# Infini-attention and a spectral filter on one core: other steps for maxima, products, keys and reciprocals, and 14 instead of 15 products in the output projection

## The chip, the cores and the metric

The kernel runs on one core of a Trainium2 chip. A core has several engines that work beside one another, each on its own queue of instructions in program order: TensorE for matrix products (PE in the profile; PEld are its weight loads), VectorE (DVE), ScalarE (ACT), GpSimd (POOL), and SyncE (SP), which here only issues DMA transfers. The engines wait for one another by semaphores. The metric is the device time of a run in microseconds; of several runs the median is given.

## The reference

Two computations share the input size of 2048 x 576 and are written side by side. The first (A) is attention with a compressive memory, with 32 heads of 18 columns and 4 segments of 512 rows:

```python
phi = lambda t: jnp.where(t > 0, t + 1.0, jnp.exp(t))
for s in range(N):                       # 4 segments
    qs, ks, vs = q[:, :, s], k[:, :, s], v[:, :, s]
    logits = jnp.einsum("bhqd,bhkd->bhqk", qs, ks) * scale + mask   # causal
    p = _softmax(logits, axis=-1)
    a_dot = jnp.einsum("bhqk,bhkd->bhqd", p, vs)
    pq = phi(qs)
    num = jnp.einsum("bhld,bhde->bhle", pq, M)
    den = jnp.einsum("bhld,bhd->bhl", pq, z)[..., None] + 1e-6
    o = g * (num / den) + (1.0 - g) * a_dot
    pk = phi(ks)
    M = M + jnp.einsum("bhld,bhle->bhde", pk, vs)
    z = z + jnp.einsum("bhld->bhd", pk)
return o @ wo
```

The second (B) is `irfft2(rfft2(x) * (w_r + 1j*w_i))` over 2048 x 576.

## The kernel before, in words

Up to about 356 us TensorE computes part B as products with Fourier tables, and, between these, the projections of part A to queries, keys and values, which go to DRAM (qkD, vD, pqD). From then on the attention loop runs, `attention`, with t from 0 to 132. A step t handles one head of one segment. k = t // 4 is a quad of four heads, hh = t % 4 the head in it, n = t // 8 a group of eight heads, and g = n // 4 the segment.

Each step interleaves three pieces of work on TensorE. `s1` multiplies queries and keys for a later step (t+10), and VectorE takes the row maxima (L647 a plain reduction over a masked product, L641 a reduction with the mask added in the same instruction, followed by a read of its accumulator). `s2` multiplies again for the step t itself (L682, L686, L687, L691), now with the maximum as two more rows of the query stack, so that ScalarE can take the exponential at once. `pv` multiplies the exponentials by the values, for two steps together (L711).

The maxima go from `s1` to `s2` by `mpath(k)`: VectorE and ScalarE gather them (L659, L660), GpSimd splits them into a high and a low half (mh, L662 and L663), TensorE transposes them (L666), ScalarE copies the result to mts (L669; there is one buffer), and two steps after that a DMA issued by ScalarE puts them into rows 108 and 109 of the query stack (L672, `Qs<-mts`). It is started for the quad k+2 at hh = 1, and its other two pieces are both taken at hh = 3.

Queries and keys of a group of eight heads come as stacks of 108 rows, six loads of 18 rows each (L621, 144 KB). There are three query stacks and four key stacks in turn (the tiles Qs, Ks, and an x that takes over an older buffer). The loads wait in a Python list q, from which two a step are issued on SP, between the smaller transfers: products out (uD, rD; L722, L727), values (L628), pq (L756). The program order of SP is the order of issue. A load of a stack that is to be used again waits until the last product on its old contents.

When a segment g-1 is complete, `recip` (L745, L749) inverts its row sums and sends them through DRAM to a tile rr; `combine` multiplies the products ux, loaded from uD by `ux_load` (L805), by rr (L826, L829, L831), adds the memory's part, and splits the result into a high part oh and a low part ol (L816, L819), in five tiles t = 0 to 4 of 126 rows, the last of 72. `mem1` (L784, L790) computes the memory's part am from pq, `den` (L765) its denominators, and `oproj` (L849) the output projection: for each of 8 units of 128 rows by 288 columns, 15 products, namely oh with the high part of wo, oh with its low part, ol with its high part, for five tiles each. `mixed` runs `combine` and `mem1` in turn. These are generators in a list bg, of which one piece a step (now and then two) is run; `den`, the parts of `recip` and the issue of loads sit in a second list, lane. For segment 3, `last_tile` and `last_proj` do the same at the end.

`late_setup` loads wo in five parts at the start of the loop (L604 on SP, L608, L609), and each wait for a free buffer holds up what SP issues next. Before the loop, `prologue` runs the first ten steps of `s1` between the products of the inverse FFT, and issues the stacks of groups 1 and 2 and the keys of group 3.

Of the kernel before, what the change touches and what calls it, by code (L numbers as in the profile page):

```python
# [102 lines left out]
class FFT:  # L103
# [178 lines left out]
    def inverse(s,yl,pp):  # L282
# [101 lines left out]
class ATT:  # L384
# [210 lines left out]
    def late_setup(s,cp):  # L595

        nc,io=s.nc,s.io; q=[]
        s.sel=cp.tile([96,5,126],BF,name="sel",bufs=1); nc.gpsimd.dma_start(s.sel,io["sel"].rearrange("p (t m) -> p t m",t=5))
        s.woh=cp.tile([126,5,576],F32R,name="woh",bufs=1); s.wol=cp.tile([126,5,576],F32R,name="wol",bufs=1)
        for t in range(6):  # L600
            if t>1: yield
            if t<5:
                x=cp.tile([128,576],F32,name="ob")[:126]; q.append(x)
                nc.sync.dma_start(x,io["wo"][:,576*t:576*t+576])  # L604
            for _ in range(2): yield
            if t>0:
                x=q.pop(0)
                nc.scalar.copy(s.woh[:,t-1],x)  # L608
                nc.gpsimd.tensor_tensor(s.wol[:,t-1],x,s.woh[:,t-1].bitcast(F32),op=OP.subtract)  # L609
        yield  # L610
        yield from s.gates()
    def stack_dmas(s,n,qk):
# [17 lines left out]
    def s1(s,t):  # L630

        nc=s.nc; k,hh=divmod(t,4); n,qd=divmod(k,2); h=4*qd+hh
        Q,K=s.Qs[n%3],s.Ks[n%4]; tp=s.sm
        assert (n,0) in s.loaded and (n,1) in s.loaded,(t,n)
        if hh==0: s.mg[k]=tp.tile([128,4,4],F32,name="mg"); s.mx[k]=tp.tile([128,4,4],F32,name="mx")
        def mm(out,i):
            nc.tensor.matmul(out,Q[:108,h,128*i:128*i+128],K[:108,h,:128*(i+1)],start=True,stop=True)  # L637
        def red(src,i):
            w=128*(i+1)
            junk=tp.tile([128,512],BF,name="junk",bufs=1)  # L640
            nc.vector.tensor_tensor_reduce(out=junk[:,:w],in0=src,in1=s.mask[:,512-w:],scale=1.0,scalar=-3.0e38,  # L641
                op0=OP.add,op1=OP.max,accum_out=s.mg[k][:,hh,i:i+1])
# [4 lines left out]
        nc.vector.tensor_reduce(out=s.mx[k][:,hh],in_=pa.rearrange("p (b c) -> p b c",c=128),axis=mybir.AxisListType.X,op=OP.max)  # L647
# [158 lines left out]
    def combine(s,g):  # L806

        nc=s.nc; tp=s.tp; xs=s.ux
        s.oh=[None]*5; s.ol=[None]*5
        eng=lambda: nc.vector if s.now>=117 else nc.gpsimd  # L810
        yield
        yield
        def high(u):
            r=126 if u<4 else 72
            s.oh[u]=tp.tile([126,512],F32R,name="oh",bufs=5); s.ol[u]=tp.tile([126,512],F32R,name="ol",bufs=5)
            (nc.vector.tensor_copy if s.now>=119 else nc.scalar.copy)(s.oh[u][:r],s.am[u][:r])  # L816
        def low(u):
            r=126 if u<4 else 72
            eng().tensor_tensor(s.ol[u][:r],s.am[u][:r],s.oh[u][:r].bitcast(F32),op=OP.subtract)  # L819
        late=g==2  # L820
        for t in range(7+late):
            if t>1 and not late: high(t-2); low(t-2)
            if t<5:
                r=126 if t<4 else 72; x=xs[t]
                pb=s.post("pb")
                nc.tensor.matmul(pb[:r],s.sel[:,t,:r],s.rc["rr"],start=True,stop=True)  # L826
# [7 lines left out]
            if late and 1<t<7: high(t-2)  # L834
            if late and t>2: low(t-3)
            yield
    def oproj(s,g):
        nc=s.nc
        oh,ol=s.oh,s.ol
        for tb in range(4):  # L840
            ob=s.tp.tile([128,576],F32,name="ob")
            c=slice(128*tb,128*tb+128)
            for hf in range(2):
                ps=(s.ps.tile([128,512],F32,name="po",tag=s.potag) if s.potag else s.post("po"))[:,:288]
                w=slice(288*hf,288*hf+288)
                L=[(a,b,t) for a,b in ((oh,s.woh),(oh,s.wol),(ol,s.woh)) for t in range(5)]
                for i,(a,b,t) in enumerate(L):
                    r=126 if t<4 else 72
                    nc.tensor.matmul(ps,a[t][:r,c],b[:r,t,w],start=i==0,stop=i==14)  # L849
# [42 lines left out]
    def prologue(s):  # L892

        nc,io=s.nc,s.io
        yield
        s.load_v(0)
        q=s.stack_dmas(1,0)+s.stack_dmas(1,1)+s.stack_dmas(2,0)+s.stack_dmas(2,1)+[lambda: s.load_v(1)]+s.stack_dmas(3,1)
        for i in range(2): yield
        i=0
        for t in range(10):  # L900
            for _ in s.s1(t):
                for _ in range(1+(i%24==0)):
                    if q: q.pop(0)()
                i+=1
                yield
            if 2<=t<6: nc.gpsimd.dma_start(s.Ks[t-2][108:110].rearrange("p h c -> p (h c)"),io["neg1"])
            if t in (3,7): m=s.mpath(t//4); next(m)
            if t in (4,8): next(m); next(m,None)
        assert not q
    def homes(s):  # L910

        for n,t,b in (("oh",F32R,5),("ol",F32R,5),("am",F32,5),("pq",F32,5),("ux",F32,3)): s.tp.tile([128 if b==3 else 126,512],t,name=n,bufs=b)
    def attention(s,tp,ps):
        nc=s.nc; s.tp,s.ps,s.psm,s.mtag=tp,ps,s.ps1,"s1"
        s.homes()
# [4 lines left out]
        m=None  # L920
# [12 lines left out]
        for t in range(133):  # L933
            k,hh=divmod(t,4); n,qd=divmod(k,2); g=k//8
            if hh==0 and qd==0:
                if 0<n<14: q+=s.stack_dmas(n+2,0)
                if 0<n<13: q+=s.stack_dmas(n+3,1)
                if n+2<16: q.append(lambda n=n: s.load_v(n+2))
            st=t%32
            if 16<=t<21: s.pq_load(1,t-16)  # L940
            if t==34: bg.append(s.den(1,lane))
            if st==8 and g>0:
                def ln(g=g):
                    r=s.recip(s.rD[g-1],s.rrD[g-1],s.g1,False,"rr",2)
# [12 lines left out]
            if qu: qu.pop(0)()  # L957
# [88 lines left out]
def arrays(x,wq,wk,wv,wo,beta):  # L1046
    f=lambda a: np.asarray(a,np.float32)
    return dict(xa=host_xa(f(x)),wqk=host_wt(np.concatenate([f(wq),f(wk)],1)).reshape(128,-1),wv=host_wt(f(wv)).reshape(128,-1),
        wo=host_wo(f(wo)).reshape(126,-1),beta=np.repeat(f(beta),4).reshape(128,1),**atables())
# [74 lines left out]
```

## Time and profile before

| | us |
|---|---|
| median of 3 runs | 722.68 |
| lowest, highest run | 722.34, 756.58 |
| the profiled execution | 718.92 |
| its span, from the first to the last instruction | 717.2 |
| TensorE busy in that span | 684.1 |
| granted TensorE clock, mean | 0.997 |

The page and the answers of the trace come from the one profiled execution, so that sums are made against its 718.92 us. In its rows L12 is line 12 of the kernel. A row of the timeline gives the start, the duration, the engine, the line, the operation and its tiles (out<-in), and in brackets the idle time ahead of it with what ended it. A row of the groups of waits says which instruction of which line waited for which, with the sum, how often, and the longest. A row of the chain gives the start, the length and the work that was waited for. The table of stretches gives busy times between two points of time.

### The profile page before, as it was taken

The numbers are of one execution on the slowest core, as the hardware profiler recorded it, in microseconds if no ns is written. First come the engines' busy times: TensorE is split into PE (matmuls) and PEld (weight loads), VectorE is DVE, ScalarE is ACT, GpSimd is POOL, SyncE is SP. The second block draws the span as 40 slices with busy tenths as digits, with TensorE's granted clock in tenths as the row PEclk, the third lists the DMA queues.
The fourth block names the chain that finished last, engine by engine and source line by source line (L and its number), as shares of the span: only waits on it lengthen the run. The fifth ranks groups of instructions, "written<-read, shape, count | busy, mean of one in ns | idle before, by whom it ended". The sixth has DMA issues, their size and how long they took to land. (4 is left out here: it accounts for less than half of the span.)

```text
span 717.2 us, 14460 instructions
## 1 busy us (share of the span) xinstructions
PE 684.1 (95%) x5007; PEld 505.7 (71%) x5007; DVE 552.3 (77%) x1270; ACT 450.1 (63%) x985; POOL 211.1 (29%) x403
## 2 busy tenths in 40 slices
PE   4999999999999999999999899899999999999997
PEld 4988869879779879999854444444466445664497
DVE  5999979899699789788588787878466876568633
ACT  3665796585586575444487677767466776567521
POOL 5432000100200111665154333435123662235300
PEclk9999999999999999999999999999999999999999
DMA  8995435645363568899547665776446775441152
GB/s 305 293 280 164 148 118 185 192 169 182 110 220 147 178 198 281 208 231 228 165 111 174 171 172 136 185 173 170 114 126 158 195 169 126 126 137 42 28 153 83
DMA packets 83304, 121.02 MB, mean 169 GB/s; under 512 B 11472, under 2 KB 50750, under 8 KB 83096
## 3 DMA queue, kind: packets, MB, share of 16 engines
q1 hardware_dynamic: 76580, 104.11, 50.3%
q0 software_dynamic: 5632, 15.76, 8.0%
q8 instruction: 39, 0.64, 0.4%
q10 hardware_dynamic: 1020, 0.25, 0.2%
q14 instruction: 33, 0.27, 0.1%
HBM read 81.78 MB, written 38.24 MB: 167 GB/s over the span
## 5 line engine op out<-in xcount | busy, mean ns | idle before, releaser
L641 DVE CUSTOM_DVE_ANT_0 junk<-s,x 128x512 bf16<-128x512 f32 (+1 forms) x256 | 141.4, 552 | 67.2 <-PE s L637 62.0
L696 POOL TENSOR_SCALAR_AFFINE_SELECT P<-P 128x512 f32<-128x512 f32 (+2 forms) x132 | 78.8, 623 | 67.3 <-ACT P L683 51.8
L647 DVE TENSOR_REDUCE mx<-s 128x4 f32<-128x512 f32 x128 | 87.7, 686 | 2.9 <-PE s L646 0.7
L683 ACT ACTIVATE P<-s 128x512 f32<-128x512 f32 x128 | 76.4, 597 | 16.5 <-PE s L682 5.4
L711 PE MATMUL pv<-P,vs 128*32 128x512 f32 (+3 forms) x1024 | 82.8, 441 | 0.0
L692 ACT ACTIVATE P<-s 128x256 f32<-128x256 f32 x128 | 49.4, 386 | 49.7 <-PE s L691 49.6
L688 ACT ACTIVATE P<-s 128x512 f32<-128x512 f32 x128 | 76.1, 594 | 2.0 <-PE s L687 1.8
L637 PE MATMUL s<-Ks,Qs 108*128 108x384 bf16 (+3 forms) x256 | 69.1, 301 | 1.2 <-DVE mx L647 0.9
L711 PEld LDWEIGHTS pv<-P,vs 128*32 128x32 f32 x1024 | 27.2, 109 | 45.3 <-issue 42.5
L459 PE MATMUL pj<-x,wqkh 128*128 128x512 f32 x162 | 56.5, 409 | 0.0
L205 DVE TENSOR_TENSOR Z<-t,t 128x290 f32<-128x290 f32 (+1 forms) x96 | 48.4, 554 | 0.1
L637 PEld LDWEIGHTS <-Qs 108*128 108x128 bf16 x320 | 31.5, 98 | 22.6 <-issue 11.3
L506 POOL MEMSET vt<- 128x32 f32 x16 | 2.4, 166 | 149.1 <-PE pm L516 127.7
L205 DVE TENSOR_TENSOR t<-Z 128x580 f32<-128x580 f32 x64 | 46.0, 755 | 0.0
L142 PE MATMUL f<-ftab,eh 128*128 128x290 f32 (+1 forms) x160 | 32.5, 322 | 12.1 <-DMA ftab<-ftab 9.5
L646 PE MATMUL s<-tri,idb 128*128 128x128 bf16 x256 | 43.2, 220 | 0.0
L295 PE MATMUL i<-civ,Y 128*128 128x256 f32 (+1 forms) x288 | 39.0, 288 | 0.2 <-POOL Y L280 0.2
L295 PEld LDWEIGHTS i<-civ,Y 128*128 128x128 f32 (+1 forms) x288 | 36.4, 181 | 1.0 <-POOL Y L280 0.4
L306 PE MATMUL i<-itab,T 128*128 128x290 f32 (+1 forms) x224 | 36.3, 305 | 0.1
L637 PE MATMUL s<-Ks,x 108*128 108x384 bf16 (+3 forms) x128 | 35.3, 306 | 1.1 <-DVE mx L647 0.6
L142 PEld LDWEIGHTS f<-ftab,eh 128*128 128x128 f32 (+1 forms) x160 | 26.2, 207 | 14.1 <-issue 8.5
L459 PE MATMUL pj<-x,wqkl 128*128 128x512 f32 x90 | 35.5, 395 | 0.0
(203 smaller groups left out, 1820.8 us busy)
## 6 DMA issues: line engine op xcount, KB each, us to landing
qkD<-sp SPq DMA_DIRECT2D x36, 384.0 KB
Ks<-qkD SPq DMA_DIRECT2D x72, 144.0 KB
x<-qkD SPq DMA_DIRECT2D x60, 144.0 KB
Qs<-qkD SPq DMA_DIRECT2D x60, 144.0 KB
xin<-xb SPq DMA_DIRECT2D x16, 384.0 KB
cfw<-cfw POOLq DMA_DIRECT2D x16, 384.0 KB, 4.4
civ<-civ POOLq DMA_DIRECT2D x16, 384.0 KB, 7.6
vs<-vD SPq DMA_DIRECT2D x16, 330.0 KB
```

Source lines behind the costliest of these rows:

```text
L142: nc.tensor.matmul(p[:,r,:FP],x,t,start=n==0,stop=n==6)
L205: v.tensor_tensor(o,a,b,op=op)
L295: nc.tensor.matmul(p[:m,k],Y[i][:,q,c*128:c*128+m],cc[:,hl,o:o+256],start=n==0,stop=n==5)
L459: s.nc.tensor.matmul(out,a,b,start=i==0,stop=i==len(L)-1)
L637: nc.tensor.matmul(out,Q[:108,h,128*i:128*i+128],K[:108,h,:128*(i+1)],start=True,stop=True)
L641: nc.vector.tensor_tensor_reduce(out=junk[:,:w],in0=src,in1=s.mask[:,512-w:],scale=1.0,scalar=-3.0e38, op0=OP.add,op1=OP.max,accum_out=s.m ...
L647: nc.vector.tensor_reduce(out=s.mx[k][:,hh],in_=pa.rearrange("p (b c) -> p b c",c=128),axis=mybir.AxisListType.X,op=OP.max)
L683: nc.scalar.activation(P[0][:,hh],p0,AF.Exp,scale=SC)
L688: nc.scalar.activation(P[1][:,hh],p1,AF.Exp,scale=SC)
L692: nc.scalar.activation(P[2][:,hh],p2,AF.Exp,scale=SC)
L696: nc.gpsimd.affine_select(out=x[:,r],in_=x[:,r],pattern=[[0,r.stop-r.start],[1,128]],compare_op=OP.is_ge,fill=0.0,base=0,channel_multiplie ...
L711: nc.tensor.matmul(s.pvt[32*hh:32*hh+32,128*j:],vt[:,j,19*h:19*h+32],mv[0][:,hh,mv[1]],start=j==0,stop=j>1,skip_group_check=True)
```

## The change

- **Lead.** `s1` runs 11 steps ahead instead of 10, and `prologue` runs 11 steps of it. The keys of group 3 are loaded in the first steps of the loop instead of in `prologue`.
- **Reductions.** In `s1` for t from 11 to 14, the two reductions with the mask inside are plain ones; the mask is added by a product on TensorE.
- **Maxima.** `mpath(k+2)` starts at hh = 0 and its other two pieces are taken at hh = 1, one step later instead of two. The transfer to the query stack is thus issued two steps earlier.
- **Products' loads.** The first three `ux_load` of a segment are issued during three of the steps of `recip` instead of together after them. Tile 4, that of 72 rows, becomes the first in the loads of pq, in `mem1`, in `combine` and in `ux_load`.
- **Denominators.** For segments 2 and 3, `den(g+1)` comes after the first four pieces (two units) of `oproj(g-1)` rather than ahead of it.
- **Projection.** The 72 rows of tile 4 leave 56 free. The tile oh[4] gets 56 rows of the low part below its own, ol[4] becomes oh once more with the remaining 16 rows of the low part below, and the operands of wo are stacked to fit. Tile 4 then takes two products instead of three, and a unit 14 instead of 15. Three transfers within SBUF per segment put the rows in place, one and two steps later. wo is loaded in six parts of 128 rows. Segment 3 keeps its products.

```diff
@@ tables and setup
+ORD=(4,0,1,2,3)
 def host_wo(w):
-    o=np.zeros((126,5,D),np.float32)
-    o[:,:4]=w[:504].reshape(4,126,D).transpose(1,0,2)
-    o[:72,4]=w[504:]
+    o=np.zeros((128,6,D),np.float32)
+    o[:126,:4]=w[:504].reshape(4,126,D).transpose(1,0,2)
+    o[:72,4]=w[504:]; o[72:,4]=w[504:560]; o[72:88,5]=w[560:]
...
-        for t in range(6):
-            if t>1: yield
-            if t<5:
-                x=cp.tile([128,576],F32,name="ob")[:126]; q.append(x)
+        for t in (0,1,2,3,5,4,6):
+            if t: yield
+            if t<6:
+                x=cp.tile([128,576],F32,name="ob"); q.append((t,x))
                 nc.sync.dma_start(x,io["wo"][:,576*t:576*t+576])
...
+                if u==5: nc.scalar.copy(s.wol[64:96,4],x[64:96]); continue
+                r=128 if u<4 else 72
+                nc.scalar.copy(s.woh[:,u],x)
+                nc.gpsimd.tensor_tensor(s.wol[:r,u],x[:r],s.woh[:r,u].bitcast(F32),op=OP.subtract)
@@ s1
         def red(src,i):
             w=128*(i+1)
+            if 11<=t<15:
+                nc.tensor.matmul(src[:,w-128:w],s.idb,s.tri,start=False,stop=True,skip_group_check=True)
+                nc.vector.tensor_reduce(out=s.mg[k][:,hh,i:i+1],in_=src,axis=mybir.AxisListType.X,op=OP.max)
+                return
@@ mixed
-                for _ in s.mem1(g,i-d): yield
+                for _ in s.mem1(g,ORD[i-d]): yield
@@ combine
+            A,B=s.oh[u],s.ol[u]
+            l=B if u<4 else tp.tile([128,512],F32R,name="ol4",bufs=1)
+            eng().tensor_tensor(l[:r],s.am[u][:r],A[:r].bitcast(F32),op=OP.subtract)
+            if u==4:
+                s.later(1,lambda: nc.sync.dma_start(B[:72].bitcast(F32),A[:72].bitcast(F32)))
+                s.later(2,lambda: (nc.sync.dma_start(A[72:128].bitcast(F32),l[:56].bitcast(F32)),nc.sync.dma_start(B[72:88].bitcast(F32),l[56:72].bitcast(F32))))
...
-            if t>1 and not late: high(t-2); low(t-2)
+            if t>1 and not late: high(ORD[t-2]); low(ORD[t-2])
...
-                if t<2: s.later(1,lambda t=t: s.ux_load(g,t+3))
+                if t<2: s.later(1,lambda t=t: s.ux_load(g,ORD[t+3]))
@@ oproj
-                L=[(a,b,t) for a,b in ((oh,s.woh),(oh,s.wol),(ol,s.woh)) for t in range(5)]
+                L=[(a,b,t,126) for a,b in ((oh,s.woh),(oh,s.wol),(ol,s.woh)) for t in range(4)]+[(oh,s.woh,4,128),(ol,s.wol,4,88)]
...
-                    if i==7: yield
+                    if i==6: yield
@@ prologue
-        q=s.stack_dmas(1,0)+s.stack_dmas(1,1)+s.stack_dmas(2,0)+s.stack_dmas(2,1)+[lambda: s.load_v(1)]+s.stack_dmas(3,1)
+        q=s.stack_dmas(1,0)+s.stack_dmas(1,1)+s.stack_dmas(2,0)+s.stack_dmas(2,1)+[lambda: s.load_v(1)]
...
-        for t in range(10):
+        for t in range(11):
@@ attention
-                if 0<n<13: q+=s.stack_dmas(n+3,1)
+                if n<13: q+=s.stack_dmas(n+3,1)
...
-            if 16<=t<21: s.pq_load(1,t-16)
+            if 16<=t<21: s.pq_load(1,ORD[t-16])
...
                     for i in range(8):
+                        if 2<i<6: s.ux_load(g-1,ORD[i-3])
                         next(r); yield
-                    for u in range(3): s.ux_load(g-1,u)
                     yield from r
                     bg.append(s.mixed(g))
-                    if g<3: bg.append(s.den(g+1,lane))
-                    bg.append(s.oproj(g-1))
+                    o=s.oproj(g-1)
+                    if g<3: bg.append(itertools.islice(o,4)); bg.append(s.den(g+1,lane))
+                    bg.append(o)
...
-            a=s.s1(t+10) if t+10<128 else iter(())
+            a=s.s1(t+11) if t+11<128 else iter(())
...
-            if hh==3 and m is not None: steps(m,1)
+            if hh==1 and m is not None: steps(m,1)
             steps(b,1)
-            if hh==3 and m is not None: steps(m,1)
-            if hh==1 and k+2<32: m=s.mpath(k+2); next(m)
+            if hh==1 and m is not None: steps(m,1)
+            if hh==0 and k+2<32: m=s.mpath(k+2); next(m)
```

More of the change, by code (lines that the diff above doesn't have):

```diff
@@ L1 @@
-import math
+import math, itertools
 from contextlib import ExitStack
@@ L598, in late_setup @@
         s.sel=cp.tile([96,5,126],BF,name="sel",bufs=1); nc.gpsimd.dma_start(s.sel,io["sel"].rearrange("p (t m) -> p t m",t=5))
-        s.woh=cp.tile([126,5,576],F32R,name="woh",bufs=1); s.wol=cp.tile([126,5,576],F32R,name="wol",bufs=1)
-        for t in range(6):
-            if t>1: yield
-            if t<5:
-                x=cp.tile([128,576],F32,name="ob")[:126]; q.append(x)
-                nc.sync.dma_start(x,io["wo"][:,576*t:576*t+576])
[L605 to L609, printed above, removed]
+        s.woh=cp.tile([128,5,576],F32R,name="woh",bufs=1); s.wol=cp.tile([128,5,576],F32R,name="wol",bufs=1)
+        for t in (0,1,2,3,5,4,6):
+            if t: yield
+            if t<6:
+                x=cp.tile([128,576],F32,name="ob"); q.append((t,x))
+                nc.sync.dma_start(x,io["wo"][:,576*t:576*t+576])
+            yield
+            if t!=5: yield
+            if len(q)>(t<6):
+                u,x=q.pop(0)
+                if u==5: nc.scalar.copy(s.wol[64:96,4],x[64:96]); continue
+                r=128 if u<4 else 72
+                nc.scalar.copy(s.woh[:,u],x)
+                nc.gpsimd.tensor_tensor(s.wol[:r,u],x[:r],s.woh[:r,u].bitcast(F32),op=OP.subtract)
         yield
@@ L814, in high @@
             r=126 if u<4 else 72
-            s.oh[u]=tp.tile([126,512],F32R,name="oh",bufs=5); s.ol[u]=tp.tile([126,512],F32R,name="ol",bufs=5)
+            s.oh[u]=tp.tile([128,512],F32R,name="oh",bufs=5); s.ol[u]=tp.tile([128,512],F32R,name="ol",bufs=5)
             (nc.vector.tensor_copy if s.now>=119 else nc.scalar.copy)(s.oh[u][:r],s.am[u][:r])
@@ L832, in combine @@
                     eng().tensor_tensor(s.am[t][:r],x[:r],s.am[t][:r],op=OP.add)
-                if t<2: s.later(1,lambda t=t: s.ux_load(g,t+3))
-            if late and 1<t<7: high(t-2)
-            if late and t>2: low(t-3)
+                t=i
+                if t<2: s.later(1,lambda t=t: s.ux_load(g,ORD[t+3]))
+            if late and 1<t<7: high(ORD[t-2])
+            if late and t>2: low(ORD[t-3])
             yield
@@ L845, in oproj @@
                 w=slice(288*hf,288*hf+288)
-                L=[(a,b,t) for a,b in ((oh,s.woh),(oh,s.wol),(ol,s.woh)) for t in range(5)]
-                for i,(a,b,t) in enumerate(L):
-                    r=126 if t<4 else 72
-                    nc.tensor.matmul(ps,a[t][:r,c],b[:r,t,w],start=i==0,stop=i==14)
-                    if i==7: yield
+                L=[(a,b,t,126) for a,b in ((oh,s.woh),(oh,s.wol),(ol,s.woh)) for t in range(4)]+[(oh,s.woh,4,128),(ol,s.wol,4,88)]
+                for i,(a,b,t,r) in enumerate(L):
+                    nc.tensor.matmul(ps,a[t][:r,c],b[:r,t,w],start=i==0,stop=i==13)
+                    if i==6: yield
                 nc.scalar.copy(ob[:,w],ps)
@@ L910, in homes @@
     def homes(s):
-        for n,t,b in (("oh",F32R,5),("ol",F32R,5),("am",F32,5),("pq",F32,5),("ux",F32,3)): s.tp.tile([128 if b==3 else 126,512],t,name=n,bufs=b)
+        for n,t,b in (("oh",F32R,5),("ol",F32R,5),("am",F32,5),("pq",F32,5),("ux",F32,3),("ol4",F32R,1)): s.tp.tile([128 if n in ("oh","ol","ux","ol4") else 126,512],t,name=n,bufs=b)
     def attention(s,tp,ps):
@@ L1048, in arrays @@
     return dict(xa=host_xa(f(x)),wqk=host_wt(np.concatenate([f(wq),f(wk)],1)).reshape(128,-1),wv=host_wt(f(wv)).reshape(128,-1),
[L1049 removed]
+        wo=host_wo(f(wo)).reshape(128,-1),beta=np.repeat(f(beta),4).reshape(128,1),**atables())
 def emit(nc,tc,io):
```

3 lines of the change are left out of this document (1 added, 2 removed).

## The prediction

> **What bounds the kernel now.** I began with the first part of the profile's page (busy time, share of the span and instruction count of each engine), because it says which engine a saving has to reach.
>
> ```profile
> PE 684.1 (95%) x5007; PEld 505.7 (71%) x5007; DVE 552.3 (77%) x1270; ACT 450.1 (63%) x985; POOL 211.1 (29%) x403
> ```
>
> TensorE works for 684.1 us of a span of 717.2, so everything that can be gained by removing waits is 33 us. The next view is the table of stretches: start and end, length, busy time of PE, PEld, DVE, ACT, POOL, granted clock, share of the DMA engines, GB/s.
>
> ```profile
> 250.00:358.00 108.00, 107.37 (x778) 98.26 (x777) 86.61 (x192) 55.24 (x126) 40.15 (x66) 1.00 0.79 221
> 357.00:371.00 14.00, 12.87 (x106) 6.73 (x106) 12.45 (x40) 11.13 (x27) 6.35 (x11) 1.00 0.39 109
> 371.00:402.00 31.00, 28.30 (x259) 14.43 (x258) 24.69 (x79) 22.77 (x56) 14.61 (x25) 1.00 0.71 171
> 434.00:472.00 38.00, 35.22 (x318) 17.61 (x318) 32.32 (x96) 28.05 (x71) 13.97 (x31) 1.00 0.67 162
> 472.00:500.00 28.00, 26.30 (x207) 13.18 (x208) 21.84 (x64) 20.30 (x48) 12.58 (x20) 1.00 0.70 176
> 590.00:650.00 60.00, 59.91 (x515) 38.17 (x508) 38.16 (x112) 38.10 (x92) 19.02 (x40) 1.00 0.46 123
> ```
>
> Before 358 (the FFT) and after 590 TensorE is full: there only less TensorE work is a gain. It idles 1.1 us in 357 to 371, where VectorE is nearly full (12.45 of 14), and 2.7, 2.8 and 1.7 us in the three rows from 371 to 500, where the DMA share is near 0.7. The groups of waits from 358 on say what ended those idle times (microseconds, times, longest).
>
> ```profile
> PEld L682 <- DMA Qs<-mts: 3.7, 3, 1.6
> PE s L682 <- DMA Qs<-mts: 3.2, 3, 1.4
> ACT mts L669 <- DMA Qs<-mts: 2.6, 3, 1.3
> PE pd L765 <- DMA pq<-pqD: 1.4, 1, 1.4
> PE pb L826 <- DMA rr<-rrD: 1.2, 1, 1.2
> PEld L637 <- DMA Qs<-qkD: 1.1, 2, 0.7
> PE s L637 <- DMA Qs<-qkD: 0.4, 1, 0.4
> ```
>
> PEld and PE rows of one line are the same stall twice, so I count PE's 3.2 and a wait of 0.25 us of the same kind at 406.96: about 3.5 us for the maxima. The other two removable waits are 1.4 and 1.2 us. The chain of work that ended last shows the transfers themselves (start, length, what).
>
> ```profile
> 387.69 5.19 DMA pq<-pqD
> 392.89 8.27 DMA Qs<-qkD
> ...
> 460.61 5.79 DMA rr<-rrD
> ...
> 467.94 8.14 DMA Ks<-qkD
> ...
> 481.35 8.42 DMA Qs<-mts
> ...
> 500.58 6.41 DMA pq<-pqD
> ```
>
> A maxima transfer of 8 KB takes 8.42 us, as long as the 144 KB of a query part (8.27). The time is not in the bytes: a transfer stands behind those issued before it. In 371 to 500 the loads are a line in which each new one waits its turn.
>
> **The change part by part.** *Reductions of steps 0 to 3.* They run where VectorE is the limit.
>
> ```profile
> 356.18 0.69 DVE L647 TENSOR_REDUCE mx<-s 128x4 f32<-128x512 f32 x1
> 356.79 0.68 DVE L641 CUSTOM_DVE_ANT_0 junk<-s,x 128x512 bf16<-128x512 f32 x1
> 357.39 0.08 DVE L641 DVE_READ_ACCUMULATOR2_ANT mg<- 128x1 f32 x1
> 357.62 0.42 DVE L641 CUSTOM_DVE_ANT_0 junk<-s,x 128x256 bf16<-128x256 f32 x1
> 357.97 0.69 DVE L647 TENSOR_REDUCE mx<-s 128x4 f32<-128x512 f32 x1
> ```
>
> From start to start, a plain reduction over 512 takes 0.61 us (356.18 to 356.79) and the custom one with its accumulator read 0.83 (to 357.62): 0.22 saved, four times, is 0.9; for the four over 256 (0.35 to the next start) I see nothing to save. Eight mask products are added on TensorE, which idles only 1.1 us there. Range 0 to -0.9; I take **-0.5**.
>
> *Lead 11 instead of 10.* One more step of maxima work goes into the FFT stage and leaves the end of the loop. Both stretches are full on TensorE, so it is the same work at another place: 0. VectorE has room before 358 (86.61 of 108). The six key loads that leave the prologue fall into 357 to 371, where the DMA share is 0.39: 0. But each query stack is now wanted one step sooner, while its loads are put into the queue at the same step as before, since the buffer is free no earlier. Here are the first uses in the program's TensorE order (start, length, operation, idle time before it).
>
> ```profile
> 398.77 0.33 PE L637 MATMUL s<-Ks,x 108*128 108x384 bf16 x1
> 401.64 0.34 PE L637 MATMUL s<-x,Qs 108*128 108x384 bf16 x1
> ...
> 468.58 0.33 PE L637 MATMUL s<-Ks,Qs 108*128 108x384 bf16 x1
> 471.98 0.34 PE L637 MATMUL s<-x,Qs 108*128 108x384 bf16 x1 [0.44 <-DMA Qs<-qkD]
> ```
>
> The first pair is around group 4, the second around group 8. The last query load of group 4 lands at 392.89 + 8.27 = 401.16 in the chain and its stack's first use is at 401.64; at 471.98 the matmul waits for the load itself. There is no spare time at either place. In the changed kernel the step that began at 398.77 wants what lands at 401.2 to 401.6, and the one that began at 468.58 wants what lands near 471.9. If the line of loads moves at its own pace, TensorE is late by 2.4 to 2.9 us at the first and, less the 0.44 already waited and some 0.5 of other work between, by **+2.4** at the second. These are not added: the second is where TensorE stands in relation to the loads, whatever was won earlier. That is the point on which my sum turns: the gains ahead of 472 (0.5 at the start, the maxima at 380, 398 and 407, the 1.2 for rr at 466) are swallowed, because TensorE arrives earlier only to wait for the same load. Lower bound: 0, if the loads land as much earlier as TensorE comes.
>
> *Maxima two steps earlier.* The transfer is issued about 4 us sooner, as two steps take:
>
> ```profile
> 412.95 1.21 PE pv L711 x16
> ...
> 416.99 1.21 PE pv L711 x16
> ```
>
> One such group of products is emitted per two steps. The largest wait for maxima is 1.6 us, so all go: -3.5 at most, of which only the one at 489.8 (0.8 us) lies behind 472, and there the next query stack is again close; I count 0 of it. The copy to mts still waits for the previous transfer out of its single buffer (2.6 us in the waits), as the distance between two copies stays; ACT is 63% busy and the wait doesn't pass on unless the exponentials behind it come late.
>
> The price is a new near-wait. The transposition of the maxima (L666) came two steps after the instructions that feed it, now one.
>
> ```profile
> 384.36 0.69 DVE L647 TENSOR_REDUCE mx<-s 128x4 f32<-128x512 f32 x1
> ...
> 385.80 0.42 DVE L641 CUSTOM_DVE_ANT_0 junk<-s,x 128x256 bf16<-128x256 f32 x1
> ...
> 384.82 0.22 POOL L663 TENSOR_TENSOR mh<-mg,mh 128x16 bf16<-128x16 f32 x1
> 386.23 1.42 POOL L609 TENSOR_TENSOR wol<-ob,woh 126x576 fp32r<-126x576 f32 x1 [1.19 <-ACT woh L608]
> ...
> 387.57 0.22 PE L666 MATMUL mt<-idb,mh 128*128 128x128 bf16 x1
> ```
>
> In this pattern the reductions of the even step end at 385.80 + 0.42 = 386.2. The two operations on POOL end 0.8 us after the last reduction (385.04 after 384.2), so 387.1 in the new order, against a transposition at 387.57: 0.5 us to spare, where there were 2.5. A POOL operation of 1.42 us or an additional VectorE one of 0.69 ahead of it uses that up. Behind a late transposition TensorE's whole in-order queue waits. Bounds: 0, and 30 times 0.9 (1.42 less 0.5) = 27; nearer the first, since these operations are few and the steps with combine work are longer: **+0.5**.
>
> *ux loads earlier, tile 4 first.* Three loads leave the place right before the rr load in SP's queue. The wait of 1.2 at 466.44 goes; it is swallowed as said. The ux loads themselves then lie beside query loads some eight steps earlier: bytes as before, 0.
>
> *den after two units of oproj.* The wait of pd on pq (1.4 us at 507.13, end of the chain's 500.58 + 6.41) gets two units of 15 matmuls, each over 1.9 us, ahead of it. It goes: **-1.4**. It lies behind 472, so it is kept.
>
> *14 products instead of 15.* Here is how five matmuls stand in the undisturbed part:
>
> ```profile
> 682.37 0.83 PE L849 MATMUL po<-woh,ol 126*128 126x288 f32 x5
> 683.03 0.83 PE L849 MATMUL po<-woh,oh 126*128 126x288 f32 x5
> 683.70 0.83 PE L849 MATMUL po<-wol,oh 126*128 126x288 f32 x5
> ```
>
> Five in 0.667 us is 0.133 each; a product fewer in 8 units of 3 segments is 24 x 0.133 = 3.2 us. Two segments lie within the loop with TensorE the limit: 2 x 1.07. The third is in the tail, where the last segment's reciprocal is being waited for, so I count 0.6 of its 1.07: **-2.7**. The three added small transfers per segment go out on SP one and two steps after the subtraction, with tile 4 now the first of the five; between them and their use lie the other four tiles. 0; if they are late, one wait of a transfer's 5 to 8 us per segment, 15 to 25 in all, which I hold for unlikely for that distance.
>
> The Trainium skill, page *DMA: Bandwidth & Descriptors*, section "Anatomy of one DMA — SWDGE (gpsimd) path", gives a transfer about 2.0 us fixed and its bytes at 436 GB/s. By that, an estimate, 144 KB would take 2.3 us and six such loads would be there long before their use, so the query waits would not appear: the sum would be that of the first rival below. The trace disagrees in this stretch: 8.27 us for one load, at 171 GB/s. The same page, section "Why a DMA increments its semaphore by 16 and not by 1", spreads a transfer over the largest number up to 16 that divides the slowest dimensions of both sides; for blocks of 18 rows that would be 9 engines, which fits a DMA share of 0.7 in a stretch where loads queue.
>
> **Sum.** At 472 +2.4; then -1.4, -2.7 and +0.5: **-1.2**, so 717.7 for a profiled execution against 718.92. The median of the runs is 722.68, 0.52% above the profiled one, so 717.7 x 1.0052 = **721.5**. A measurement of this kernel can tell about 2% (14.5 us) from no change; this is far inside it.
>
> **The rivals.** *One: the query loads keep pace.* TensorE waits less, so buffers come free sooner, loads go out sooner, and the load line is not a limit of its own. Then all gains stay: -0.5 - 3.5 - 1.2 - 1.4 - 2.7 = -9.3, that is 709.6 or about 713.3 on the median's scale. For it speaks that the DMA share is 0.6 to 0.7 and not 1; against it the transfers of 8 us and the loads landing within half a microsecond of their use at two groups.
>
> *Two, on the slower side: the transposition comes late.* A segment's combine puts 10 operations on POOL or VectorE; over three segments some 15 quads fall beside them. If half of the quads wait 0.9 us, that is 8 x 0.9 = 7.2 in place of 0.5: +5.5, 724.4, about 728.2 on the median's scale. It decides from a loss of 1.7 us on, that is from two such waits more than I count. For it: 0.5 us to spare, and an in-order TensorE. Against: VectorE is idle a third of the time behind 500.
>
> *Three: the change doesn't do what it says.* The single mts buffer and the line of loads hold the maxima transfers back by just as much as they are asked for earlier: then the 3.5 stays too, and with the query waits as they are the total is within 3 us of the time before, near 722.7.
>
> **How the numbers follow.** Forecast 0.45 (717 to 725 on the median's scale), rival one 0.3, two 0.2, three 0.05. The range reaches from a little below rival one, 711, to a little above rival two, 730. To be faster by over 2% the kernel would have to lose half of all TensorE idle time: 0.03. Slower by over 2% would take 16 late transpositions, or late transfers for the stacked operands in two segments: 0.05.
>
> **What would show it.** Right: no wait of the score matmul (now L690) on maxima; new waits of L641 on query loads, near steps 21 and 53, of 2 to 3 us; no wait on rr or pq; 112 products per segment in the projection. Wrong: no wait of L641 on query loads (rival one), or a matmul of the transposition (L674) waiting on POOL's mh in several quads (rival two). The whole would be wrong if the stacked transfers made the projection wait, or if the earlier traffic of 357 to 371 held up the query loads of group 3.

## The result, and the profile after

The changed kernel takes 729.19 us (median of 6 runs, 727.66 to 732.2) against 722.37 for the kernel before: a ratio of 1.0125, 95% interval 1.0079 to 1.0171. It is slower by 1.25%: less than 2%, but clear of noise. (One run of the kernel before, of 756.58 us, lies far above the other five and is left out of the ratio.) Its profiled execution has a span of 725.9 us against 717.2. First the busy times of its page:

```profile
PE 684.2 (94%) x4991; PEld 503.4 (69%) x4991; DVE 552.0 (76%) x1262; ACT 451.3 (62%) x986; POOL 209.2 (29%) x403
```

TensorE's sum is what it was (684.1), so the 8.7 us are idle time or slower products. The stretches of the changed kernel that answer to those of before:

```profile
357.00:371.00 14.00, 11.20 (x94) 6.31 (x93) 11.61 (x28) 9.19 (x23) 4.57 (x9) 1.00 0.68 162
371.00:402.00 31.00, 27.01 (x224) 13.35 (x224) 20.83 (x64) 22.48 (x54) 13.80 (x22) 0.89 0.62 155
402.00:418.00 16.00, 13.24 (x121) 6.69 (x123) 11.71 (x40) 10.24 (x26) 5.26 (x11) 1.00 0.70 168
434.00:472.00 38.00, 33.79 (x287) 16.39 (x280) 27.17 (x81) 24.70 (x61) 12.45 (x29) 0.91 0.63 152
590.00:650.00 60.00, 59.86 (x503) 36.81 (x496) 38.66 (x114) 39.23 (x94) 22.54 (x43) 1.00 0.51 139
```

TensorE idles 2.8, 4.0 and 4.2 us in the rows from 357, 371 and 434, against 1.1, 2.7 and 2.8 before. The column of the granted clock has 0.89 and 0.91 where it had 1.00. The groups of waits of the changed kernel say what ended the idle times (L641 is the product for the maxima, L690 the first score product, L674 the transposition):

```profile
PE s L641 <- DMA ux<-uD: 3.8, 1, 3.8
PE s L690 <- ACT P L691: 2.7, 5, 1.7
PE mt L674 <- POOL mh L671: 2.6, 5, 0.8
PE s L641 <- DMA x<-qkD: 2.5, 1, 2.5
```

No wait of L690 on maxima is left, and the products that waited for rr and pq (now L839 and L773) wait for them no more. In their place stand waits of L641 on query loads. The name in the first row misleads: several transfers raise the same semaphore in turn, and the row names one that was issued after the load in question. That ux load goes out only at 461.40; the product needs a query stack, whose last load lands at 462.00, and starts at 462.14. This is a wait of that kind in TensorE's timeline of the changed kernel, at step 13, and the clock around it in its table of stretches:

```profile
383.56 0.27 PE L699 MATMUL s<-Qs,Ks 110*128 110x256 bf16 x1
386.33 0.50 PE L641 MATMUL s<-Ks,x 108*128 108x384 bf16 x1 [2.50 <-DMA x<-qkD]
...
388.37 2.36 PE L719 MATMUL pv<-P,vs 128*32 128x512 f32 x16
...
394.11 1.28 PE L719 MATMUL pv<-P,vs 128*32 128x384 f32 x16
```
```profile
383.00:386.50 3.50, 1.00 (x7) 0.48 (x6) 1.80 (x6) 1.91 (x6) 3.50 (x5) 0.88 0.82 171
386.50:388.00 1.50, 1.50 (x7) 0.77 (x6) 0.69 (x1) 0.38 (x1) 0.49 (x3) 0.50 0.85 193
390.00:392.00 2.00, 2.00 (x20) 1.21 (x13) 0.43 (x2) 0.52 (x2) 0.00 (x0) 0.50 0.54 181
394.00:398.00 4.00, 4.00 (x42) 2.04 (x40) 3.55 (x14) 3.87 (x9) 2.40 (x4) 1.00 0.49 148
```

Sixteen products that take 1.28 us undisturbed take 2.36 behind the wait (both groups stream 5120 columns in all): from the wait until 392.5, some 6 us, TensorE runs at half its clock. The wait costs about twice what its row says. The same stands behind the 1.42 us wait on pq in the kernel before, which the prediction priced at 1.4 (timeline, then stretch):

```profile
507.13 1.02 PE L765 MATMUL pd<-pq,zst 72*32 72x512 f32 x2 [1.42 <-DMA pq<-pqD]
...
510.53 1.74 PE L711 MATMUL pv<-P,vs 128*32 128x384 f32 x16
```
```profile
509.00:511.00 2.00, 2.00 (x12) 0.76 (x13) 1.39 (x3) 1.06 (x3) 0.55 (x1) 0.50 0.42 121
```

The Trainium skill, page *TensorE: Matmul & The Clock Gate*, section "What's actually happening", has the clock halved after at least one idle window of about 3.4 us. The halving is in the trace; the idle times ahead of it were shorter, 2.5 and 1.4 us, so the measurement decides.

To see where time goes I also compared, step by step, when the first score product of step t starts. This is not a view of the profile but worked out from its rows; each column is the delay against the kernel before, in us:

```
step            0     12     15     21     45     48     66     69     87    127
changed       1.6    2.5    7.9    8.5   11.5   13.6   12.2    8.9    8.9    8.7
```

From step 0 to 12 the delay grows by 1 us, around the waits at steps 13 and 45 by 5.4 and some 5, den's change gives 3.3 back at step 66, and the rest is small. A warning belongs to this table: the kernel in which den alone was moved is the same program as before up to step 66, and its trace was behind by 5.3 us more at step 30 than at step 0. What a single trace shows below that needs runs.

### The profile page after: what moved, and what is told of

It is laid out like the page before. It is cut to its first block, busy times and chain, and to the rows that moved or that the text cites. A ratio compares the mean times of both kernels' runs of the same rounds, so it can differ in the third digit from the quotient of the medians.

```text
span 725.9 us, 14435 instructions
## 1 busy us (share of the span) xinstructions
PE 684.2 (94%) x4991; PEld 503.4 (69%) x4991; DVE 552.0 (76%) x1262; ACT 451.3 (62%) x986; POOL 209.2 (29%) x403
## 4 chain that ended last, share of the span: by engine, by line
PE 65%; DMA 9%; ACT 5%; DVE 3%; POOL 2%; issue 2%; SPq 1%; ACTq 0%; POOLq 0%; DVEq 0%
PE pj L460 12%; PE pv L719 8%; PE s L641 8%; PE pjv L460 8%; PE po L862 5%; PE i L295 4%; PE i L306 4%; PE s L690 3%; PE s L694 2%; PE pn L792 2%; PE pm L517 2%; PE s L654 2%; PE s L699 1%; DMA pq<-pqD 1%; DMA x<-qkD 1%
## 5 line engine op out<-in xcount | busy, mean ns | idle before, releaser
L649 DVE CUSTOM_DVE_ANT_0 junk<-s,x 128x512 bf16<-128x512 f32 x248 | 137.0, 552 | 66.5 <-PE s L641 61.9
L691 ACT ACTIVATE P<-s 128x512 f32<-128x512 f32 x128 | 77.6, 606 | 25.6 <-PE s L690 11.6
L719 PE MATMUL pv<-P,vs 128*32 128x512 f32 (+3 forms) x1024 | 84.5, 448 | 0.0
L696 ACT ACTIVATE P<-s 128x512 f32<-128x512 f32 x128 | 77.5, 605 | 2.3 <-PE s L695 2.1
L641 PE MATMUL s<-Ks,Qs 108*128 108x384 bf16 (+3 forms) x256 | 70.0, 305 | 5.0 <-DMA ux<-uD 3.8
L641 PEld LDWEIGHTS <-Qs 108*128 108x128 bf16 x320 | 31.7, 99 | 28.8 <-issue 13.5
L641 PE MATMUL s<-Ks,x 108*128 108x384 bf16 (+3 forms) x128 | 35.7, 309 | 3.7 <-DMA x<-qkD 2.5
```

Of the source, the lines that this page charges most:

```text
L691: nc.scalar.activation(P[0][:,hh],p0,AF.Exp,scale=SC)
L696: nc.scalar.activation(P[1][:,hh],p1,AF.Exp,scale=SC)
L719: nc.tensor.matmul(s.pvt[32*hh:32*hh+32,128*j:],vt[:,j,19*h:19*h+32],mv[0][:,hh,mv[1]],start=j==0,stop=j>1,skip_group_check=True)
```

## The experiments

Ratios are to the kernel before in runs on the same chip, with 95% intervals.

**1. The lead and what goes with it undone** (the core of the edit).

```diff
-            a=s.s1(t+11) if t+11<128 else iter(())
+            a=s.s1(t+10) if t+10<128 else iter(())
...
-            if hh==0 and k+2<32: m=s.mpath(k+2); next(m)
+            if hh==1 and k+2<32: m=s.mpath(k+2); next(m)
```

> The changed kernel with the lead of 10 steps, the start and steps of the maxima, the first reductions and the place of the keys of group 3 as before; the projection in 14 products, the order of tile 4, the place of den and the ux loads stay changed. Theory A (the loss comes from query stacks wanted a step sooner: waits of 2.5 and 3.8 us at steps 13 and 45, each followed by some 5 us at half the TensorE clock, and some 4 us at the loop's start): the loss goes and the gain of den (3.3 in the step table) and of the projection (about 2) stays, 717 us beside 722.4. Rival B (the loss comes from the projection's side: a sixth part of wo that holds up SP, transfers for the stacked operands, ux loads among the query loads): it stays at 727 or above.

Measured: 719.24 us, 1.0009 (0.9971 to 1.0046). The loss is gone with the lead group; rival B falls. But the gain that I expected of den and the projection can't be measured either.

**2. The lead group alone, on the kernel before.**

> The kernel before with only the lead of 11, the earlier maxima, the plain first reductions and the keys of group 3 loaded in the loop. Theory A: slower than the changed kernel, since den's and the projection's gains are missing: about 734, with waits of the score matmul on query loads near steps 13 and 45. Rival B: 724 or below.

Measured: 731.06 us, 1.0151 (1.0089 to 1.0212). The lead group alone brings the whole loss, so rival B falls here too; which of its four parts does it, this run can't say. Whether it is slower than the changed kernel, as theory A has it, the intervals don't tell. The earlier maxima, which belong to this group, bring nothing that shows.

**3. The keys of group 3 back in the prologue.**

```diff
-        ...+[lambda: s.load_v(1)]
+        ...+[lambda: s.load_v(1)]+s.stack_dmas(3,1)
...
-                if n<13: q+=s.stack_dmas(n+3,1)
+                if 0<n<13: q+=s.stack_dmas(n+3,1)
```

> The changed kernel with the keys of group 3 loaded in the prologue again. If these six loads at the loop's start hold up ScalarE (its maxima transfer stands behind them, and TensorE waits 1.7 us for an exponential at step 4) and the query loads of group 3: 5 to 7 us less, 722 to 724, and the wait at step 13 shorter. If only ScalarE's block comes from them: about 2 less, 727. If neither: 729.

Measured: 723.5 us, 1.0059 (1.0027 to 1.0091): by the ratios some 5 us less than the changed kernel, though the two intervals still overlap a little. In its step table the start and step 13 cost next to nothing (a delay of 0.1 us at step 15); by step 21 it is 4.0, behind a wait of 3.14 us at 400.88 for ScalarE, which had stood 4.74 us at the issue of a maxima transfer.

**4. Products without use in place of the two long waits.**

```diff
+            if t in FILLS:      # {13:9, 45:14}
+                d=s.post("fl")
+                for _ in range(FILLS[t]): nc.tensor.matmul(d,s.Qs[n%3][:108,0,:128],s.Ks[n%4][:108,0,:512],start=True,stop=True)
             steps(a,1)
```

> The changed kernel with 9 products without use (108x128 by 108x512, written to a spare bank and never read) ahead of the maxima's products of step 13, and 14 at step 45, so that TensorE works through most of the two long waits. If the clock, halved after these idle times, is part of the loss: granted clock 1.00 behind both steps and 2.5 to 3 us less at each, 724 in all. If the waits alone are the loss: 729, within 1.

Measured: 726.62 us, 1.008 (1.0045 to 1.0114). That is some 3 us less by the ratios, half of what was expected, and the interval overlaps that of the changed kernel, so that runs don't show the clock's part. The trace does: the clock stays at 1.00 behind both steps, and the table has 3.2 us less at step 15. At step 21 that is gone (8.9 against 8.5): a wait of 2.88 us for ScalarE now stands at 405.75. ScalarE had stood at the issue of a maxima transfer until a pq load landed, at 404.36; in the changed kernel that load lands at 404.52, and the same product starts at 405.92. What is won at one place is lost at the next, as long as something else sets the pace.

**5 to 7. The six query loads of a group issued together**, in the changed kernel, in the kernel before, and in the changed kernel with the keys in the prologue.

```diff
-            if q: q.pop(0)()
+            for _ in range(6 if t%8==0 and 0<n<14 else 1):
+                if q: q.pop(0)()
```

> The changed kernel with all six query loads of a group put into SP's queue at the first place of the step in which their buffer comes free, instead of two a step over three steps. Theory A, sharpened (a query stack's round trip, from the step that frees its buffer to its last landing, takes some 11 us; six steps of 1.99 us covered it, five don't, and each group pays the difference): the trip gets shorter by some 2 to 4 us, the matmuls' waits on query loads at groups 3, 4, 5, 7, 8, 9 mostly go, 720 in all. Rival C (the loads are paced by the line of transfers, whatever the order of issue): landings and waits stay, 727 or more.

> The kernel before with the six query loads of a group issued together in the same way. Theory A: six steps cover the trip but at groups 4 and 8, so little is won, 719 to 721 beside 720.7. Rival C: the same, 721.

> The changed kernel with the keys of group 3 in the prologue and the six query loads issued together. Theory A: both losses go, the gains of den, projection and maxima stay: 715 to 718. Rival C: as with the keys alone, 723.

Measured: 739.24 (1.027, 1.022 to 1.0321), 748.89 (1.0385, 1.0325 to 1.0446), 738.17 (1.0247, 1.0202 to 1.0291). All three far off, and neither theory foresaw it. The trip did get shorter: in the kernel before, the loads of group 4 go out from 391.14 on and the last lands at 400.56, 9.4 us later instead of 13.5; no wait on query loads is left there. The waits of that kernel show who pays:

```profile
PE s L682 <- DMA Qs<-mts: 6.9, 6, 2.5
PE pb L826 <- DMA rr<-rrD: 6.7, 2, 5.9
PE pd L765 <- DMA pq<-pqD: 6.1, 2, 4.2
ACT P L683 <- DMA pq<-pqD: 5.3, 1, 5.3
```

The loads are one line after all. What is put ahead in it delays the small transfers behind, and ScalarE, which issues the maxima's transfers, stands still until a pq load has landed that SP issued earlier (last row). Behind these waits comes the clock, with a mean of 0.974 in place of 0.997. So C was right on the line, and A on the trip.

**8. The ux loads at their old place**, in the kernel of experiment 1.

> The kernel of the first experiment (lead 10) with the three ux loads together after eight parts of recip, as before. If the early ux loads lie among the query loads of group 8 and cost the 2.2 us that its step table shows between steps 45 and 51: 717 beside 719.2. If they only move: 719 to 720.5, with the wait on rr back.

Measured: 721.14 us, 1.0009 (0.9975 to 1.0043), as without the edit. With a lead of 10, the early ux loads cost and bring nothing that runs can tell; with a lead of 11 this was not tried.

**9. The lead of 11 alone.** On the kernel before, the two lines with 10 become 11; nothing else.

> The kernel before with a lead of 11 alone: maxima, keys of group 3, reductions, projection, den as before. Theory A (each group pays for the query stack being wanted a step sooner): waits of the score matmul on query loads at groups 3, 4, 5, 7, 8, 9, which lacked 1.2, 2.8, 2.0, 0.3, 3.3 and 1.9 us in the trace of before, 5 to 9 us in all, so 724 to 728 beside 719. Rival D (the lead costs nothing; keys at the loop's start and the maxima's shorter way cost it): 719 to 721.

Measured: 729.12 us, 1.0125 (1.0071 to 1.0178), the same ratio as the whole change. Its waits:

```profile
PE s L637 <- DMA Qs<-qkD: 8.2, 3, 3.4
PE s L637 <- DMA x<-qkD: 3.0, 1, 3.0
```

11.2 us at four places, with a clock of 0.89 and 0.88 in the stretches from 402 and 472. Rival D falls. The losses don't add up, though: the lead alone costs as much as the whole change, and the changed kernel with only its keys put back costs half of that.

**10. den after two units of the projection, alone.**

> The kernel before with den after two units of the projection and nothing else. If the wait of 1.4 us on pq counts with the half clock behind it, as the step table of the changed kernel shows (3.3 us between steps 66 and 69): 3 us faster, 716. If only the wait: 717.5. If the load lands later in its place: 719.

Measured: 718.98 us, 0.9997 (0.9959 to 1.0034). A gain of 1.4 us would be 0.2% and lies within the interval; the 3 us of the step table would be 0.4% and lie at its edge. Open.

**11. The transposition two steps after its start, in the changed kernel.**

```diff
-            if hh==1 and m is not None: steps(m,1)
+            if hh==2 and m is not None: steps(m,1)
```

> The changed kernel with the transposition of the maxima two steps after its start, as before, instead of one, and so the transfer one step earlier than before instead of two. If the late mh (TensorE waits 2.6 us for it in five places) is a loss of its own: 726 to 727. If it is hidden behind the query waits: 729, within 1.

Measured: 729.28 us, 1.0131 (1.0079 to 1.0183). The late mh is no loss of its own here.

**12 to 15. Query stacks reloaded in two halves of four heads**, each as soon as that half is free: with the lead of 11 alone, in the changed kernel, in the changed kernel with the keys in the prologue, and in the kernel before.

```diff
-                if 0<n<14: q+=s.stack_dmas(n+2,0)
+                if 0<n<14: q+=s.half_dmas(n+2,1)      # heads 4 to 7
...
+            if t%8==4 and n<13: q+=s.half_dmas(n+3,0)  # heads 0 to 3, four steps earlier
```

> The kernel before with a lead of 11 and each query stack reloaded in two halves of four heads, the first half four steps earlier. Theory A (five steps between release and first use are too few for a trip of some 11 us): no waits on query loads of over 1 us, no loss against the kernel before: 718 to 721. Rival C (the line of transfers sets the pace; more transfers make it worse): 729 or more.

> The changed kernel with query stacks reloaded in halves. Theory A: the loss of the lead goes; that of the keys in the loop stays in part: 719 to 723. Rival C: 729 or more.

> The changed kernel with query stacks reloaded in halves and the keys of group 3 in the prologue. Theory A: what is left are the gains of den, the projection and the maxima: 714 to 717. Rival C: 724 or more.

> The kernel before with query stacks reloaded in halves, lead 10: the control. Theory A: its waits on query loads (1.5 us) go, 717 to 719. Rival C: the twofold number of loads costs, 722 or more.

Measured: 720.18 (0.9991, 0.9957 to 1.0024), 727.16 (1.0093, 1.0058 to 1.0129), 724.06 (1.0056, 1.0016 to 1.0096), 720.51 (0.9991, 0.9959 to 1.0022). With the lead of 11 alone the loss is gone, with the same bytes in more transfers, and the control doesn't move: the time in which to reload was its cause. But the changed kernel keeps 0.9%, not clearly less than its 1.25%, and with the keys in the prologue 0.6%. In these two the long waits on query loads are gone too; others stand there. The waits of the kernel with halves and keys in the prologue, and ScalarE's timeline of it (L703 is the exponential, L692 the issue of the maxima's transfer):

```profile
PE s L702 <- ACT P L703: 10.1, 11, 4.8
ACT P L703 <- DMA ux<-uD: 6.6, 1, 6.6
ACT P L703 <- DMA vs<-vD: 3.3, 1, 3.3
```
```profile
477.99 0.38 ACT L712 ACTIVATE P<-s 128x256 f32<-128x256 f32 x1
484.29 0.62 ACTq L692 DMA_DIRECT2D Qs<-mts  x1
484.95 0.60 ACT L703 ACTIVATE P<-s 128x512 f32<-128x512 f32 x1 [6.58 <-DMA ux<-uD]
```

ScalarE, with exponentials to do, stands 6.58 us at the issue of a transfer of 8 KB, until a load that SP had issued lands. TensorE then waits for the exponentials.

The trace's records of the issues say why it is that load. SP and ScalarE together use eight semaphores to learn of landings, in turn, and nearly every issue first waits for the landing of the transfer that had its semaphore before, as a rule eight issues earlier. The issue at 484.29 takes the semaphore of a ux load issued at 476.23, and the last count of that load comes at 484.21. So the line of this document is, at least in part, one of eight places that the program hands out in turn; what share of the loads' 8 us comes from it was not tested.

**16 and 17. The maxima's transfers issued by GpSimd; the maxima's times as before.** Both on the kernel with halves and with the keys in the prologue.

```diff
-        else: s.later(2,lambda: nc.scalar.dma_start(out,mt))
+        else: s.later(2,lambda: nc.gpsimd.dma_start(out,mt))
```

> The changed kernel with query stacks in halves and the keys of group 3 in the prologue, the maxima's transfers issued by GpSimd instead of ScalarE. If ScalarE's block at the issue is what is left of the loss: its idle times ahead of L703 that a transfer ends (10 us in all) go, 0.994 to 0.999 of before. If the late mh (3.5 us of waits at the transposition) or the other parts hold it: 1.004 or more.

> The same kernel with the maxima's start and steps as before (hh = 1 and 3) and ScalarE as the issuer. If the earlier maxima, by either way, are what is left: 0.996 to 1.001 of before. If the other parts (projection, ux, tile 4, den) are: 1.004 or more.

Measured: 712.77 us, **0.9892** (0.985 to 0.9935), and 718.32 us, 0.9987 (0.9956 to 1.0018). Either edit takes the rest of the loss away (for the second the intervals just touch); the first gives a kernel that is faster than the kernel before, by 1.1%. GpSimd's transfers use eight semaphores of their own there, and ScalarE has none to issue. The waits of this kernel, for the same lines:

```profile
PE s L702 <- ACT P L703: 0.7, 3, 0.3
PE mt L686 <- POOL mh L683: 2.6, 6, 0.8
PE pb L851 <- DMA rr<-rrD: 0.6, 1, 0.6
```

10.1 us have become 0.7, and the transposition's 2.6 (3.5 in experiment 14) are still there and do little. The second edit's trace is less clear: TensorE still waits 6.1 us for exponentials there, and 2.8 us for maxima, so its rows don't show by which way the loss went.

**18. The same issue by GpSimd in the kernel of experiment 1** (lead 10, whole stacks).

> The kernel of the first experiment (lead 10) with the maxima's transfers issued by GpSimd rather than ScalarE, so that they neither stand in the line of SP's loads nor hold up ScalarE. If the line is what makes them late: the waits on maxima go, 716 beside 719. If GpSimd's own work or a slower path holds them back: 720 or more, with waits on maxima.

Measured: 721.0 us, 1.0018 (0.9981 to 1.0054): nothing. The issuer alone doesn't help where the maxima are asked for late; that the gain needs the earlier maxima, the halves or both was not taken apart further.

## Why the prediction was right or wrong

The forecast of 721.5 us, a hair faster, was wrong: the kernel became slower by 1.25%. The time lies within the range, close to rival two's 728.2, but that is luck: it is not by rival two's mechanism, since the transposition given back its step changed nothing (729.28).

**Query stacks.** The mechanism was named: stacks wanted a step sooner, loads released at the same step, no spare time. The places were only half right: the long waits of the changed kernel stand at steps 13 and 45, for groups 3 and 7, not near 21 and 53, for groups 4 and 8; with the lead alone, groups 4 and 8 have them too (3.40 and 3.21 us). One reading was off as well: the load that lands at 401.16 is the fifth of group 4, and the sixth lands at 401.60, 0.04 us before its stack's first use. The step that failed is "These are not added: the second is where TensorE stands in relation to the loads, whatever was won earlier", and with it "If the line of loads moves at its own pace". The loads do not run on a clock of their own. They are released by TensorE's progress. Here is the first load of group 4 in SP's timeline and the first score product of step 16, with which the stack is free, before and after:

```profile
388.11 0.97 SPq L621 DMA_DIRECT2D Qs<-qkD  x2
...
388.09 0.38 PE L682 MATMUL s<-Qs,Ks 110*128 110x512 bf16 x1
```
```profile
395.76 0.67 SPq L625 DMA_DIRECT2D Qs<-qkD  x2
...
395.90 0.38 PE L690 MATMUL s<-Qs,Ks 110*128 110x512 bf16 x1
```

TensorE is 7.8 us later and so are the loads: in the changed kernel SP stands from 394.57 on until TensorE has freed the stack, and before the change it comes to this load just as the stack is free. A group's lateness moves the next group's release, and each group pays again. Nearer to the runs comes a sum of each group's shortage: in the trace of before the stack of group m landed 9.5 to 15.5 us after the start of step 8(m-2), near 11 in most, while the first five steps took 9.2 to 11.2 us up to group 8, and 14.0 for group 9. Groups 3, 4, 5, 8 and 9 lack 0.8, 2.5, 1.5, 3.0 and 1.5 us with five steps, 9.3 in all. For the lead alone I had +2.4; it measured +1.25% or 9 us (5 to 13 by the interval). That the two agree so well is in part chance, since the halved clock after each wait, a term that I had nowhere, comes on top of the shortages.

**Keys: 0.** The stretch from 357 had room in its mean DMA share (0.39), and I took that for enough. The six loads made it 0.68, and ScalarE stood 2.25 us at its issue there:

```profile
362.45 0.38 ACT L700 ACTIVATE P<-s 128x256 f32<-128x256 f32 x1
363.79 1.24 ACTq L680 DMA_DIRECT2D Qs<-mts  x1
365.08 0.60 ACT L691 ACTIVATE P<-s 128x512 f32<-128x512 f32 x1 [2.25 <-issue]
```

With the loads back in the prologue ScalarE doesn't stand there, the wait at step 13 for the query loads of group 3 is 0.62 us instead of 2.50, and the kernel is some 5 us faster by the ratios. The prediction had named the hold-up of these query loads among its signs of being wrong, but gave it no time in the sum. A mean share doesn't say how long the line is at the moment when an urgent transfer joins it.

**Maxima: all waits go.** They did. "ACT is 63% busy and the wait doesn't pass on unless the exponentials behind it come late" is the second step that failed. I looked at the copy to mts and not at the issue itself. The issue sits on ScalarE's in-order queue and waits there for an earlier transfer to land; asked for two steps earlier, it meets the loads. Experiment 14 has 10.1 us of it at TensorE, experiment 16 has 0.7.

**mh: +0.5.** The trace has 2.6 us in five places; no cost in the runs.

**ux: 0.** Right within 0.4%, with a lead of 10; not tried with 11.

**den: -1.4; projection: -2.7.** Right in sign in the step table (3.3 at step 66, since the half clock goes too; some 2 between steps 69 and 126 without the lead group); in the tail nothing in the changed kernel and 0.9 without the lead group, where I had 0.6. In runs none of it shows: 1.0009 for all of it, 0.9997 for den alone. That fits a pace set by loads, but was not shown to come from it.

**First reductions: -0.5.** Never seen alone; the start became 1 us slower with ScalarE's block, and without it (experiment 3) it was 0.7 us faster by step 9.

Rival one's -9.3, without any wait on query loads and with the earlier maxima, lies near what a kernel reaches that nobody had asked about: with halves and GpSimd as the issuer the runs show -1.08%, 7.8 us (4.7 to 10.8). That is by another way than "the loads keep pace", so the nearness is luck.

**Loads: 2.3 us, nine engines.** The estimate of 2.3 us is for transfers issued by GpSimd, as the title of the section says that the prediction names from the Trainium skill; these loads are issued by SP. The prediction also sets a DMA share of 0.7 beside nine engines of sixteen. Nine would be a share of 0.56, so that row doesn't show them.

## What to carry to other kernels

Where a buffer is released by the consumer and refilled for a use k steps later, compare the refill's whole trip with k steps at each place; if it doesn't fit, each such round pays, and the payments add up. A transfer issued by a compute engine is a wait on that engine's in-order queue: see what stands in the line when it is issued, and which transfer has the semaphore that it will use, before moving it earlier. An idle time of TensorE of 1.4 us or more may cost twice its length.

## What the runs showed of the hardware that was not expected

- The clock granted to TensorE fell to 0.50 for 3.4 us (508.1 to 511.5) in the kernel before, 1 us after an idle time of 1.42 us had ended, and for 6.8 us (385.7 to 392.5) in the changed kernel, from within an idle time of 2.50 us on. It did not fall behind 1.40 us at 397.88 in the kernel before, 1.71 us at 365.72 in the changed kernel or 1.90 us at 411.02 in that of experiment 14.
- An issue on ScalarE's queue stood 6.58 us, until a load issued by SP had landed that had used the same semaphore.
- Issuing the same loads a few us sooner, together, cost the kernel before 3.85%.
- Twice as many loads of half the size (1.00 with the control) cost nothing.
